# Eight of sixteen input chunks transposed early into DRAM and read back

## The chip, the cores and the metric

One core of a Trainium2 chip runs the kernel. Its engines work side by side: TensorE (PE) multiplies matrices into eight banks of PSUM, VectorE (DVE) and ScalarE (ACT) compute elementwise and copy banks to SBUF, GpSimd (POOL) and SyncE (SP) issue transfers, which run on 16 shared DMA engines. Each engine takes its instructions in order and waits at one whose inputs are not there. The metric is device time in microseconds (us); lower is better.

## The reference

Two sequence models stand side by side, each on 2048 positions of 1024 channels in bf16; their outputs are concatenated.

```python
# A: long convolution
k_shift = sum over t of k_pad[:, t:t+S, :] * shift_k[:, ks-1-t]     # ks = 4
kv = k_shift * v
y = irfft(rfft(kv) * rfft(ssm_k))[:S] + kv * ssm_D
a = q * y
# B: diagonal state space
Bu = einsum("bld,pd->blp", x, B_bar)          # complex, P = 1024 states
h[t] = Lam_bar * h[t-1] + Bu[t]
b = 2 * einsum("blp,dp->bld", h, C).real + x * Dskip
out = concatenate([a, b], axis=-1)
```

## The kernel before

Everything is emitted by one list, `ORDER`: some 1500 words such as `U.6.0.0:a30p2`. A loop takes them one by one, calls the function of that name with the numbers, and hands it slots: `a` is a unit of an arena of 53 units in SBUF (2 KB per partition each), `p` a PSUM bank, `w` a slot for the transform matrices, `h` a slot for the state. A word's engine takes it after all earlier words of that engine; a slot that is given again is waited for until its last reader is through. So the list fixes the order on each engine, the order in SP's and POOL's DMA queues, and when buffers come free. Below, "PE work between two words" is counted from the PE words that stand between them in the list.

Part B works on 16 chunks of 128 positions.

- `x.i` (line 449) reads chunk i by a transposing DMA from SP's queue, 256 KB, so that channels lie on the partitions.
- `U.i.jp.jl` (line 461) multiplies it with the prepared B: 16 matmuls of 128x128 per word, eight words per chunk. `ue.i.jp` (466) copies the bank to SBUF.
- `r1.i` (479), `r2.i` (486) rotate the input into a real recurrence, `cy.i` (488, ACT) carries the last state of chunk i-1 over, `sc.i.a` (492) scans, `r3.i` (479) and `r4.i` (498) rotate back; all but `cy` are on DVE. `cy.i` needs `r4` of chunk i-1.
- `y.i.dh.part` (508 and 511) multiplies with C and adds the skip through x: four matmuls of 512 columns and one of 128. Chunk i of x is thus read twice: by U, and at the end by y. `ye` (517) copies out, `yst` (519, POOL) or `ysp` (520, SP) stores.

Before chunk 0 the matrix B is transposed on PE (`bl` loads, `bT` line 421, `bc` line 437) and C partly there (`cl`, `cT`, `cc`), partly by transposing DMA (`cx`, line 443). `eo`, `stt`, `z1`, `z2` and the words up to `exp2` build the rotation tables.

Part A is a two-stage Fourier transform over DRAM scratch. `kp`, `vp` (526 to 534) load k and v; `kvm`, `kva`, `kvb`, `kvc` (543 to 558, DVE) make kv; `am` (563) and `ae` (569) transform 16 pieces, `ast` (572, POOL) stores them. The same for ssm_k: `hl` (578) loads, `hT` (587) transposes on PE, `hc` (592) and `hm` (609), `he` (617), `hst` (620, POOL). Then, for 16 pairs of frequencies: `lw` (624) loads matrices, `lh` and `lk` (629) read the scratch, `sh`, `sk` (640), `she` (649), `ske` (656), `sw` or `swp` (660: a swap of partitions by DMA, from POOL or SP), `pr` (666, DVE: the product), `sa` (678), `sae` (686), `vst` (689, POOL). At the end `vl` (694) reads back, `qp` (699) loads q, `a3` (706) and `a3e` (713) finish, `qm` (715, DVE) multiplies by q, `ost` (716, POOL) or `osp` (717, SP) stores. A copy whose word ends in `v` (`uev`, `shev`, ...) runs on DVE instead of ACT.

The words of part A fill the gaps of part B; both run through the whole kernel.

Of the kernel before, what the change touches and what calls it, by code (L numbers as in the profile page):

```python
# [66 lines left out]
ORDER = """  # L67
bl.0.1:a46 ld_par ld_w:a0 wb.3:p0 wbe.3:a20 bl.6.0:a32 par_T:p2 p32 exp1 dd wb.6:p4 wbe.6 wb.2:p2 ld_F wbe.2 kp.0:a12
bl.7.1:a42 bl.6.1:a43 wb.1:p1 bl.0.0:a35 wb.7:p3 wbe.7 wbe.1 wb.0:p7 bT.6.0:p4 gz x.1:a48 kring bc.6.0 wbe.0
bl.7.0:a25 kp.1 wb.5:p1 wbe.5 wb.4:p5 bl.1.0:a9 bT.0.1:p4 dve2 dve3 tabA1:a4a40a6a10 wbe.4 exp2 kp.-1 bT.6.1:p1  # L70
bT.0.0:p2 x.0:a49 bc.0.1 bT.7.1:p3 bl.2.1:a42 sm_pre sin0 bT.7.0:p5 rt bc.6.1 bc.0.0 bl.3.1:a24 tabA2 bl.1.1:a33
kvm.3:a26 U.1.3.0:a34p6 bT.1.0:p4 par_rest kva.3 U.1.0.0:p2 bc.7.1 bc.7.0 U.1.3.1 U.0.3.0:a8p0 U.0.3.1 kvm.1:a44
bT.2.1:p5 sin2 bl.2.0:a43 bl.3.0:a50 sin1 bT.3.1:p7 eo bc.1.0 kvb.3:a39 bT.1.1:p3 U.0.0.0:p1 bc.2.1 bl.5.0:a30 kva.1
kvm.2:a0 stt bl.5.1:a31 kva.2 bT.2.0:p4 bl.4.1:a38 bc.1.1 bT.3.0:p5 bl.4.0:a52 ue.0.3 U.1.0.1 U.0.0.1 bc.2.0 bc.3.0
bT.4.1:p3 bT.5.0:p0 ue.1.0 bT.4.0:p5 kp.-2 U.1.1.0:p2 bc.3.1 kvm.0:a26 bT.5.1:p4 bc.5.0 bc.4.1 kvb.1:a38 kva.0 bc.4.0
cl.2.0:a32 bc.5.1 ue.0.0 U.1.1.1 U.0.1.0:p0 x.2:a51 cT.2.0:p7 kvb.2:a36 ue.1.3 U.0.1.1 U.0.2.0:p4 vp.0:a42 U.0.2.1
cc.2.0 kvb.0:a37 ue.0.1 z1 U.1.2.0:p3 ue.0.2 U.2.1.0:a30p1 U.2.1.1 ue.2.1 cl.0.0:a24 cx.5.1 kvc.1 am.1.1:p5p6
ae.1.0.1:a28 U.1.2.1 vp.1:a6 ae.1.1.1 kvc.0 ue.1.2 U.2.3.0:p5 cl.3.1:a52 cl.1.0:a33 cT.0.0:p0 am.0.1:p1p7 ue.1.1
r1.0:a0 z2 cc.0.0 hl.1.0:a44 U.2.2.0:p2 U.2.2.1 kvc.3 ae.0.0.1:a40 r2.0:h1 ae.0.1.1 ue.2.2 kvc.2 U.2.3.1 sc.0.0
am.0.0:p3p4 kp.2 cl.2.1:a42 cl.3.0:a50 hl.1.1 sc.0.1 cT.2.1:p6 x.3:a9 r1.1:a4 ae.0.1.0 r3.0:a24 cT.3.1:p7 cT.3.0:p4  # L80
U.2.0.0:p0 cc.3.1 cc.2.1 hl.0.1:a0 U.2.0.1 cx.7.1 ae.0.0.0 hl.0.0 cl.1.1:a52 cc.3.0 cx.7.0 r2.1:h0 U.3.0.0:a10p1 ast.0
r4.0 am.1.0:p2p7 lw.0:w0 cx.4.0 cl.0.1:a32 ue.2.0 U.3.1.0:p6 cx.4.1 hT.0.5:p3 U.3.1.1 ue.2.3 ae.1.1.0 cT.1.1:p4
hc.0.5:a50 U.3.3.0:p3 ae.1.0.0 hT.0.2:p0 ue.3.1 am.2.0:p5p2 cc.1.1 cy.1 r1.2:a4 hT.0.7:p7 hT.0.0:p6 U.3.2.0:p4
hc.0.2:a8 cT.0.1:p0 ae.2.0.0:a34 hc.0.0:a52 U.3.0.1 sc.1.0 ld_Q ld_sd:a37 sc.1.1 ast.1 cx.5.0 kp.3 hT.0.1:p5 hT.0.4:p6
U.3.3.1 cc.0.1 cx.6.0 r2.2:h2 ue.3.0 ae.2.1.0 U.3.2.1 hc.0.7:a38 hm.0.2.0:p1p0 hc.0.4:a43 hm.0.2.1:p2p7 ue.3.3
cT.1.0:p6 cx.6.1 he.0.2.0.0:a40 ue.3.2 r3.1:a24 cc.1.0 hc.0.1:a8 he.0.2.1.0 he.0.2.1.1 y.0.1.0:p3 y.0.1.1 hd.0 y.0.1.2
hm.0.0.1:p4p6 hm.0.0.0:p5p2 hT.0.3:p1 y.0.1.3 r4.1 he.0.0.0.1:a26 y.0.0.0:p2 he.0.0.0.0 he.0.2.0.1 hT.0.6:p7 cy.2
he.0.0.1.1 hst.0.0.0 hst.0.2.1 he.0.0.1.0 y.0.0.1 am.2.1:p6p4 kvm.4:a30 hc.0.3:a2 hst.0.2.0 hst.0.0.1 hc.0.6:a25
ae.2.0.1 y.1.0.0:p5 sc.2.1 ae.2.1.1 kvm.5:a4 ye.0.1:a24 sc.2.0 y.0.0.2 hm.0.3.1:p0p1 he.0.3.1.1:a0 vp.2:a28
hm.0.4.0:p6p4 hm.0.3.0:p7p3 kva.5 he.0.4.0.0:a2 he.0.3.1.0 lw.3:w2 y.0.0.3 kva.4 ye.0.0 kp.4 ast.2 hst.0.3.1 r3.2:a44  # L90
x.4:a52 y.1.0.1 kvb.5:a36 he.0.4.0.1 he.0.3.0.1 he.0.3.0.0 y.1.0.2 hm.0.4.1:p2p3 hm.0.5.1:p4p6 he.0.5.1.1:a26 r4.2
he.0.4.1.1 hm.0.7.1:p1p7 he.0.7.1.1:a40 y.1.0.3 kvb.4:a42 y.1.1.0:p0 he.0.4.1.0 he.0.5.1.0 ye.1.0:a49 ysp.0 y.1.1.1
hm.0.5.0:p4p2 he.0.5.0.1 kvm.8:a44 r1.3:a4 he.0.5.0.0 hm.0.6.0:p3p6 he.0.6.0.0:a34 y.1.1.2 kva.8 he.0.6.0.1 y.1.1.3
y.2.0.0:p3 am.3.0:p6p5 ae.3.1.0:a30 y.2.0.1 r2.3:h1 hm.0.7.0:p2p5 he.0.7.1.0 he.0.7.0.1 hm.0.6.1:p7p4 kvc.4 ae.3.0.0
hst.0.3.0 kvc.5 hst.0.7.1 kvb.8:a4 he.0.6.1.1 he.0.6.1.0 ye.1.1 hst.0.4.0 cy.3 yst.1 y.2.0.2 y.2.0.3 hst.0.6.1
ye.2.0:a48 hst.0.6.0 he.0.7.0.0 vp.4:a10 sc.3.0 y.2.1.0:p6 y.2.1.1 am.3.1:p5p0 hst.0.4.1 ae.3.0.1 y.2.1.2 y.2.1.3
sc.3.1 hst.0.5.0 am.4.1:p2p4 x.5:a34 ae.4.1.1:a6 hst.0.7.0 ye.2.1 ae.3.1.1 U.4.0.0:a32p7 U.4.3.0:p5 am.5.1:p1p0
kvm.6:a0 U.4.3.1 ae.5.0.1:a28 vp.3:a40 U.4.0.1 kvc.8 ast.3 ue.4.3 am.4.0:p1p3 ue.4.0 ae.4.1.0 ae.5.1.1 r3.3:a44
U.4.2.0:p4 kva.6 am.5.0:p3p5 U.4.2.1 ae.5.0.0 ae.4.0.0 am.8.1:p7p6 ae.4.0.1 am.8.0:p0p3 ae.8.1.0:a4 U.4.1.0:p1 r4.3
kvb.6:a35 yst.2 hst.0.5.1 ue.4.2 kvc.6 U.4.1.1 ae.8.1.1 ae.8.0.1 U.5.1.0:a30p3 kvm.9:a46 U.5.1.1 ae.5.1.0 y.3.1.0:p2  # L100
y.3.0.0:p6 am.6.1:p4p5 ast.4 y.3.0.1 kvm.7:a24 ue.5.1 am.6.0:p7p3 ae.6.1.0:a6 ue.4.1 ae.8.0.0 ae.6.1.1 ae.6.0.1
y.3.0.2 kva.9 y.3.0.3 kva.7 y.3.1.1 hm.0.1.1:p3p1 he.0.1.1.1:a38 hm.0.1.0:p4p5 he.0.1.0.1 ye.3.0:a35 he.0.1.1.0
he.0.1.0.0 ae.6.0.0 y.3.1.2 kvb.9:a36 kvb.7:a51 kvc.9 hl.3.1:a42 y.3.1.3 hl.3.0 ye.3.1 hl.2.1:a0 hl.2.0 U.5.2.0:p1
am.9.1:p6p3 ae.9.0.1:a8 ae.9.1.1 U.5.2.1 ue.5.2 hT.1.3:p2 kvc.7 ast.5 hc.1.3:a50 kp.5 r1.4:a46 am.7.0:p6p5 hT.1.0:p7
hst.0.1.0 ae.7.0.0:a32 ae.7.1.0 ast.6 kvm.11:a24 ast.8 am.9.0:p0p4 ae.9.1.0 r2.4:h0 kva.11 hc.1.0:a28 hT.1.1:p1
hT.1.5:p6 am.7.1:p5p2 hc.1.1:a29 ae.7.1.1 cy.4 sc.4.0 kvb.11:a40 U.5.3.0:p3 ysp.3 hd.1 ae.7.0.1 U.5.0.0:p4 ae.9.0.0
# [16 lines left out]
ast.12 ae.13.0.0:a48 ae.13.1.0 sc.5.1 ue.7.2 kvb.14:a24 U.7.3.0:p1 U.7.3.1 kvc.15 ue.7.3 ae.13.1.1 am.15.0:p3p0 kvc.14
am.15.1:p7p4 ae.15.1.1:a4 ae.15.0.0 ae.15.1.0 r3.5:a12 x.10:a52 r4.5 U.9.2.0:a32p1 r1.6:a20 ae.15.0.1 r1.7:a28
U.9.3.0:p6 am.14.1:p3p2 U.9.3.1 am.14.0:p7p4 r2.6:h2 ae.14.1.1:a16 ysp.4 ae.14.0.1 y.5.0.0:p0 ae.14.0.0 y.5.1.0:p7
lh.0:a0 y.5.1.1 U.9.2.1 ae.14.1.0 y.5.1.2 y.5.0.1 ae.13.0.1 ast.10 sh.7:p2p5 cy.6 ast.15 ue.9.3 ue.9.2 sh.2:p6p1
# [64 lines left out]
def full_kernel(ctx, tc, A_q, A_k, A_v, A_shift_k, A_ssm_k, A_ssm_D, B_x, B_Lre, B_Lim, B_Bre, B_Bim,  # L191
# [255 lines left out]
    def x_(i):  # L447
        st["xT", i] = sb(1).rearrange("p (d t) -> p d t", d=ND)
        nc.sync.dma_start_transpose(st["xT", i], x[i * T:(i + 1) * T, :])
# [332 lines left out]
```

## Time and profile before

| | |
|---|---|
| three runs | 357.69, 358.66, 360.29 us; median 358.66 |
| the profiled execution | 358.65 us, of which 356.8 are the span of its instructions |
| granted clock of TensorE | 0.99 |
| busy: PE, DVE, ACT, POOL | 333.2, 330.3, 271.5, 68.9 us |
| DMA | 100.91 MB, mean 283 GB/s |

The page lists busy time by engine, by fortieths of the span and by line. A busy PE is not PE at its peak: the rows of its instructions overlap, so its pace is read from the starts of dense rows. The clock is a share of full speed; the chain of waits follows the last instruction back to what released it. "SPq" is SP's DMA queue.

### The profile page before, as it was taken

What the parts mean: (1) busy time and instruction counts of PE and PEld (TensorE: products, weight loads), DVE (VectorE), ACT (ScalarE), POOL (GpSimd) and SP (SyncE); (2) the same over time, 40 slices, a digit from 0 to 9 for tenths busy, and PEclk for the clock granted to TensorE, in tenths of its full rate; (3) what the DMA queues carried; (4) which work ended last, traced back from release to release, by engine and by line L of the source; (5) the groups of instructions that cost most, each with busy time, mean ns of one, the idle gap of its engine ahead of it and who ended that gap; (6) DMA issues with size and microseconds to landing.
All of it is one profiled execution on the core that took longest, in us unless ns stands there. A gap on an engine that the chain in (4) does not pass through costs nothing.

```text
span 356.8 us, 9113 instructions
## 1 busy us (share of the span) xinstructions
PE 333.2 (93%) x3745; PEld 223.9 (63%) x3785; DVE 330.3 (93%) x277; ACT 271.5 (76%) x512; POOL 68.9 (19%) x108
## 2 busy tenths in 40 slices
...
GB/s 224 326 279 310 248 242 281 194 253 44 298 294 317 282 260 177 193 312 222 348 246 311 305 303 275 317 366 320 359 303 344 319 314 327 296 355 386 204 401 154
DMA packets 62565, 100.91 MB, mean 283 GB/s; under 512 B 29438, under 2 KB 31502, under 8 KB 62524
## 3 DMA queue, kind: packets, MB, share of 16 engines
...
q0 software_dynamic: 9840, 33.74, 26.0%
...
HBM read 52.08 MB, written 33.55 MB: 240 GB/s over the span
## 4 chain that ended last, share of the span: by engine, by line
PE 70%; DMA 12%; ACT 7%; issue 5%; SPq 3%; POOL 1%; DVE 1%; POOLq 0%; DVEq 0%
PE bank L508 25%; PE bank L461 24%; PE bank L640 4%; PE bank L678 4%; DMA arena<-in_B_x_dram 3%; DMA wslot<-a_c_W 3%; PE bank L706 3%; PE bank L563 3%; SPq L443 3%; ACT BT L437 2%; PE bank L609 2%; PE bank L511 2%; DMA arena<-Vs 2%; DMA CT<-in_B_C_im_dram 2%; PE bank L421 1%
## 5 line engine op out<-in xcount | busy, mean ns | idle before, releaser
L461 PE MATMUL bank<-arena,BT 128*128 128x128 bf16 x2048 | 129.2, 222 | 5.1 <-DMA arena<-in_B_x_dram 3.5
L461 PEld LDWEIGHTS <-BT 128*128 128x128 bf16 x2048 | 120.1, 99 | 19.5 <-issue 7.7
L508 PE MATMUL bank<-CT,gslot 128*128 128x512 bf16 x483 | 120.5, 379 | 3.0 <-issue 1.0
L492 DVE TENSOR_TENSOR_SCAN gslot<-rtab,gslot 128x1040 bf16<-128x1040 f32 x32 | 73.0, 2312 | 6.3 <-ACT gslot L488 6.2
L508 PEld LDWEIGHTS <-gslot 128*128 128x128 bf16 x512 | 44.5, 98 | 53.0 <-issue 8.7
L466 ACT CAST arena<-bank 128x512 bf16<-128x512 f32 x64 | 38.7, 623 | 19.5 <-PE bank L461 17.5
L569 ACT CAST arena<-bank 128x512 bf16<-128x512 f32 x64 | 35.9, 620 | 8.9 <-PE bank L563 8.7
L617 ACT CAST arena<-bank 128x512 bf16<-128x512 f32 x64 | 34.3, 616 | 6.9 <-PE bank L609 5.9
L666 DVE TENSOR_TENSOR arena<-arena 128x4096 bf16<-128x4096 bf16 x16 | 36.6, 2287 | 2.1 <-DMA arena<-arena 1.0
L479 DVE TENSOR_TENSOR arena<-arena,Z 128x4096 bf16<-128x4096 bf16 x16 | 36.5, 2284 | 1.1 <-ACT arena L466 1.1
L479 DVE TENSOR_TENSOR arena<-gslot,Z 128x4096 bf16<-128x4096 bf16 x16 | 36.6, 2286 | 0.4
L686 ACT CAST arena<-bank 128x512 bf16<-128x512 f32 x60 | 33.4, 610 | 4.4 <-PE bank L678 4.3
L656 ACT CAST arena<-bank 128x512 bf16<-128x512 f32 x58 | 33.0, 614 | 2.6 <-PE bank L640 2.4
L649 ACT CAST arena<-bank 128x512 bf16<-128x512 f32 x57 | 31.5, 615 | 4.4 <-PE bank L640 4.4
L620 POOL DMA_DIRECT2D Ys_h<-arena x32 | 23.3, 730 | 45.8 <-ACT arena L617 45.8
L517 ACT CAST arena<-bank 128x512 bf16<-128x512 f32 x31 | 18.8, 606 | 15.6 <-PE bank L511 15.6
L543 DVE TENSOR_TENSOR arena<-arena 128x4096 bf16<-128x4096 bf16 (+3 forms) x16 | 30.1, 1884 | 0.4 <-ACT arena L466 0.3
L511 PE MATMUL bank<-Dd,arena 128*128 128x128 bf16 x128 | 28.0, 219 | 0.2
L572 POOL DMA_DIRECT2D Ys_kv<-arena x16 | 11.2, 719 | 84.2 <-ACT arena L569 82.2
L660 POOL DMA_DIRECT2D arena<-arena x16 | 8.8, 553 | 82.9 <-ACT arena L649 44.9
L713 ACT CAST arena<-bank 128x512 bf16<-128x512 f32 x24 | 12.8, 597 | 12.1 <-PE bank L706 10.9
L511 PEld LDWEIGHTS <-arena 128*128 128x128 bf16 x128 | 12.5, 98 | 15.1
(102 smaller groups left out, 383.3 us busy)
## 6 DMA issues: line engine op xcount, KB each, us to landing
...
Ys_h<-arena POOLq DMA_DIRECT2D x32, 256.0 KB, 4.0
...
```

The costliest lines, as they stand in the source:

```text
L461: nc.tensor.matmul(pu[:, w, jl, :], BT[:, 2 * jp + jl, w, d, :], xT[:, d, :], start=(d == 0), stop=(d == ND - 1))
L466: either("ue", lambda cp, i, jp: cp(st["u", i][:, :, 2 * jp:2 * jp + 2, :], st.pop(("pu", i, jp))))
L479: nc.vector.tensor_mul(m, s_, win(Z))
L492: nc.vector.tensor_tensor_scan(gf, rtab[:].rearrange("p j t -> p (j t)"), gf, 0.0, ALU.mult, ALU.add)
L508: nc.tensor.matmul(py, h[:, w, j, 2:GW], CT[:, j, w, dh * 512:(dh + 1) * 512], start=(j == 0 and w == 0), stop=False)
L511: nc.tensor.matmul(py[:, part * P:(part + 1) * P], st["xT", i][:, d, :], Dd[:, d, :], start=False, stop=(part == 3))
L569: cp(st["ysb", n2][:, p, dh * 512:(dh + 1) * 512], st.pop(("pa", n2, p, dh)))
L617: cp(o, st.pop(("pb", hf, s, e, r)).rearrange("p (n c t) -> p n c t", n=2, c=2))
L649: cp(st["hab", i][:, 0, a, l, :], st.pop(("ps", "h", g, l)))
L656: cp(st["x16", i][:, a, l, :], st.pop(("ps", "k", g, l)))
L666: nc.vector.tensor_mul(hab, st.pop(("x16", i)).rearrange("p a l d -> p (a l d)").unsqueeze(1).to_broadcast([P, 2, 2 * D]), hab)
L686: cp(st["vsb", i][:, a, dh * 512:(dh + 1) * 512], st.pop(("pv", g, dh)))
```

## The change

For chunks 8 to 15 the transposing read `x.i` writes a buffer that is only stored, by `xs.i` on POOL's queue, to a DRAM scratch of its own. Later `xl.i` on SP's queue reads it back plainly, 256 KB, into the slot that U and y read. `x.i` and `xs.i` stand early in the list, `xl.i` shortly before chunk i. Chunks 0 to 7 are read as before. All words of `ORDER` have a new place and new slots; the arithmetic is the same. Eight `xl` and eight `xs` come in; four swaps and six y stores move from SP to POOL and two stores of the last stage the other way; 28 copies of banks run on DVE instead of 26.

```diff
+    bounced = set(map(int, re.findall(r"\bxl\.(\d+)", ORDER)))
+    xd = {i: tc.dram_tile([P, D], BF16, name="xd%d" % i) for i in sorted(bounced)}
+
     def x_(i):
+        nm = "xm" if i in bounced else "xT"
+        st[nm, i] = sb(1).rearrange("p (d t) -> p d t", d=ND)
+        nc.sync.dma_start_transpose(st[nm, i], x[i * T:(i + 1) * T, :])
+    E["x"] = x_
+    E["xs"] = lambda i: gpd(xd[i], st.pop(("xm", i)).rearrange("p d t -> p (d t)"))
+
+    def xl(i):
         st["xT", i] = sb(1).rearrange("p (d t) -> p d t", d=ND)
-        nc.sync.dma_start_transpose(st["xT", i], x[i * T:(i + 1) * T, :])
-    E["x"] = x_
+        spd(st["xT", i].rearrange("p d t -> p (d t)"), xd[i])
+    E["xl"] = xl
```

Of the list, the places that the prediction speaks of; the old ones first:

```diff
...
-ast.7 kvm.10:a24 hst.0.1.1 sc.4.1 U.5.0.1 U.5.3.1 hc.1.5:a41 hm.1.1.0:p5p2 kva.10 hm.1.1.1:p0p7 x.8:a11 ue.5.0 kp.6
-x.9:a36 U.8.0.0:a6p1 he.1.1.1.0:a46 hT.1.4:p0 hT.1.7:p6 he.1.1.0.1 U.8.3.0:p4 ue.5.3 hc.1.4:a51 he.1.1.1.1 vp.5:a48
-x.6:a10 he.1.1.0.0 U.8.3.1 kvc.11 hT.1.2:p0 hc.1.7:a29 hT.1.6:p3 hm.1.7.0:p7p5 kvb.10:a37 he.1.7.0.1:a32 he.1.7.0.0
-hc.1.2:a3 U.8.1.0:p2 U.8.1.1 ue.8.3 r3.4:a42 U.8.0.1 am.11.0:p6p5 U.6.1.0:a38p7 ae.11.1.0:a4 U.6.1.1 hc.1.6:a35 ue.8.0
...
-a3ev.10.0 ysp.13 r3.15:a10 a3ev.3.0 r4.15 a3.11.0:p7 a3.1.1:p5 a3.15.0:p3 a3.1.0:p4 a3.5.0:p6 ye.14.0:a42 a3e.15.0
-qm.1 a3ev.11.0 a3ev.5.0 y.15.1.0:p3 a3.12.1:p0 a3ev.12.1:a10 qm.5 a3.13.0:p1 a3ev.1.1 a3e.1.0 a3.13.1:p2 a3.0.0:p7
-qm.7 qm.2 a3e.0.0 a3e.13.1 a3e.13.0 y.15.1.1 a3.12.0:p0 ost.5 y.15.1.2 a3.8.0:p5 ost.2 y.15.0.0:p6 y.15.1.3 a3e.12.0
-a3.9.1:p0 a3.9.0:p4 a3.8.1:p1 qm.0 a3e.8.0:a28 a3e.8.1 a3e.9.1 qm.6 osp.1 y.15.0.1 a3ev.9.0 y.15.0.2 y.14.1.0:p1 ost.0
-qm.4 y.15.0.3 yev.15.0:a3 osp.7 ye.15.1 osp.6 y.14.1.1 ost.4 y.14.1.2 y.14.1.3 ysp.15 ye.14.1 yst.14
...
+he.0.5.0.1 ye.0.1 hm.0.4.0:p3p2 kp.4 kvc.5 r3.2:a0 hst.0.2.0 hst.0.2.1 yst.0 x.13:a11 hst.0.0.1 hm.0.4.1:p7p1
+hm.0.0.0:p0p6 he.0.4.1.0:a48 he.0.4.1.1 y.1.1.0:p5 y.1.0.3 he.0.4.0.0 kvm.8:a42 he.0.0.0.0 vp.4:a40 r4.2 y.1.1.1
+he.0.0.0.1 hm.0.5.1:p0p7 hm.0.7.0:p1p6 he.0.4.0.1 hst.0.0.0 kva.8 kvm.9:a0 y.1.1.2 he.0.5.1.0 x.4:a28 he.0.7.0.0
+hst.0.6.0 y.1.1.3 he.0.5.1.1 he.0.7.0.1 kva.9 hst.0.7.0 U.4.2.0:a36p2 hst.0.4.1 kvb.8:a38 x.5:a29 hst.0.5.1 kvb.9:a25
...
+hm.1.0.0:p6p2 he.1.0.0.0:a48 lw.0:w1 he.1.0.1.1 hm.1.1.1:p4p1 he.1.1.1.1 he.1.0.0.1 U.5.0.0:p3 hT.1.3:p6 hc.1.3:a51
+ye.3.0 x.10:a8 U.5.0.1 vp.5:a24 kvc.11 xs.10 he.1.1.1.0 ue.5.0 lw.1:w2 kp.6 ast.7 he.1.0.1.0 sc.4.0 sc.4.1 kvc.10
+hT.1.5:p1 hc.1.5:a33 hT.1.6:p5 U.8.2.0:a10p2 U.8.2.1 ue.8.2 hc.1.6:a32 U.8.0.0:p0 hT.1.7:p3 hc.1.7:a8 am.11.1:p6p7
+ae.11.1.1:a44 ae.11.0.1 hT.1.2:p4 U.8.0.1 ue.8.0 am.11.0:p5p1 ae.11.0.0 hc.1.2:a9 ae.11.1.0 U.8.1.0:p2 U.8.1.1 ue.8.1
+U.8.3.0:p3 hm.1.3.1:p4p1 he.1.3.1.0:a40 yst.3 r1.5:a0 hm.1.7.1:p5p7 he.1.7.1.1:a38 hm.1.7.0:p0p6 he.1.7.0.0 he.1.7.1.0
+hst.1.0.0 he.1.7.0.1 x.6:a27 U.6.0.0:a30p2 U.6.0.1 ue.6.0 ast.11 he.1.3.1.1 hst.1.0.1 hm.1.3.0:p5p4 he.1.3.0.0 r3.4:a4
...
+sh.7:p0p4 sh.6:p6p7 yst.4 sh.2:p5p1 she.2.0 U.9.3.0:p2 U.9.3.1 r1.7:a17 she.6.0:a4 she.6.1 r4.6 sw.0.0 y.5.0.3
+U.9.1.0:p5 r2.7:h1 U.9.1.1 ye.5.0 ue.9.3 she.2.1 she.7.1 sk.2:p6p2 cy.7 ue.9.1 ske.2.1:a24 sw.1.0 sw.1.1 sk.3:p7p1
+ske.3.1 y.6.1.0:p3 y.6.1.1 y.6.0.0:p2 y.6.1.2 swp.0.1 ske.3.0 sc.7.1 ske.2.0 sc.7.0 she.7.0 lk.0:a10 sk.0:p4p6 pr.1
...
+sae.27.0:a45 qp.6:a38 sa.26:p0p5 sae.26.1 sae.26.0 sae.27.1 vst.13 y.12.1.1 y.12.1.2 y.12.1.3 ye.12.1:a11 qp.0:a50
...
+ue.15.3 sc.14.1 sc.14.0 a3.11.0:p2 y.13.1.1 a3.7.0:p4 a3.7.1:p6 U.15.1.1 y.13.1.2 a3e.7.0:a28 a3.10.1:p4 y.13.1.3
...
+y.14.1.3 a3.8.0:p6 a3.3.0:p4 vl.1:a32 ye.12.0 vl.9:a46 a3e.12.1 y.14.0.1 qm.6 y.14.0.2 r3.15:a20 qp.4:a34 r4.15
+a3.1.1:p0 a3e.3.1 osp.2 ye.14.1:a10 a3e.3.0 a3e.8.0:a16 osp.6 qm.1 yst.12 a3.0.0:p4 osp.1 a3e.1.1:a44 a3.1.0:p5
+a3.0.1:p7 a3ev.1.0 a3.8.1:p6 a3ev.0.1 a3e.0.0 qm.0 a3.9.0:p3 a3ev.9.0 qm.5 osp.5 a3ev.8.1 ost.0 y.14.0.3 ye.14.0
+ysp.14 a3.9.1:p1 a3ev.9.1 qm.4 ost.4 y.15.1.0:p4 y.15.1.1 y.15.1.2 y.15.1.3 yev.15.1:a52 y.15.0.0:p0 y.15.0.1 y.15.0.2
+y.15.0.3 ye.15.0 yst.15
```

213 lines of the change are left out of this document (102 added, 111 removed).

## The prediction

> **What bounds the kernel now.** I read the page's busy shares first, then busy time by stretch, then who waits for whom, then the chain that ended last around the one long transfer in it, and last the rows of single lines.
>
> ```profile
> span 356.8 us, 9113 instructions
> PE 333.2 (93%) x3745; PEld 223.9 (63%) x3785; DVE 330.3 (93%) x277; ACT 271.5 (76%) x512; POOL 68.9 (19%) x108
> ```
>
> Two engines are nearly full, TensorE (PE) and VectorE (DVE). The stretches say where each has room (columns: us, then busy us of PE, PEld, DVE, ACT, POOL, the granted clock, the DMA share, GB/s):
>
> ```profile
> 60.00:120.00 60.00, 58.33 (x559) 36.17 (x566) 58.09 (x47) 46.99 (x88) 16.11 (x23) 1.00 0.75 239
> 120.00:140.00 20.00, 16.42 (x241) 14.82 (x240) 19.49 (x18) 14.20 (x26) 3.57 (x5) 0.91 0.94 240
> 140.00:180.00 40.00, 39.47 (x463) 27.27 (x467) 38.73 (x29) 32.67 (x67) 14.82 (x21) 1.00 0.78 250
> 180.00:240.00 60.00, 59.37 (x636) 34.77 (x645) 56.28 (x31) 48.79 (x100) 7.09 (x12) 1.00 0.96 309
> 240.00:300.00 60.00, 58.84 (x779) 37.96 (x786) 57.73 (x39) 53.93 (x109) 14.06 (x23) 1.00 0.93 325
> 300.00:335.00 35.00, 33.94 (x274) 19.79 (x276) 34.58 (x22) 15.61 (x31) 1.88 (x3) 1.00 0.90 328
> ```
>
> From 140 to 335 us PE is idle 3.4 us (195 less 191.6), DVE 7.7 us. PE sets the pace there; a PE stall before 140 is not won back. There is one, at 120 to 140: 3.6 us idle at a clock of 0.91. DVE is idle 10.1 us from 60 to 335.
>
> ```profile
> PE bank L461 <- DMA arena<-in_B_x_dram: 3.5, 2, 3.3
> DVE gslot L492 <- ACT gslot L488: 6.2, 6, 2.7
> 122.53 12.00 DMA arena<-in_B_x_dram
> 134.58 3.53 PE L461 MATMUL bank<-arena,BT 128*128 128x128 bf16 x32 [3.29 <-DMA arena<-in_B_x_dram]
> 138.44 1.95 PE L461 MATMUL bank<-arena,BT 128*128 128x128 bf16 x32
> 114.85 1.48 SPq L449 DMA_TRANSPOSE arena<-in_B_x_dram  x1
> 117.11 4.74 SPq L449 DMA_TRANSPOSE arena<-in_B_x_dram  x1
> 122.53 1.85 SPq L449 DMA_TRANSPOSE arena<-in_B_x_dram  x1
> L449 SPq DMA_TRANSPOSE arena<-in_B_x_dram x16: 1231/1721/5196, 4.9 to 286.7; - x16
> DMA to landing us min/median/max: 5.8/7.1/8.0
> ```
>
> The three L449 rows are x.8, x.9 and x.6, in the order's sequence. x.9 is not read until chunk 9, yet it holds SP's queue 4.74 us, and x.6 goes out behind it and takes 12.0 us. PE stands 3.29 us for x.6, and its next 32 matmuls take 3.53 us instead of 1.95, at half clock.
>
> **The change, part by part.**
>
> *The stall.* In the new order x.8 and x.9 leave this place; chunk 8 comes by xl.8, x.6 follows x.10, vp.5, lw.1 and kp.6, and its slot 27 is freed by hm.1.1.1. Between hm.1.1.1 and U.6.0.0 PE has nine U halves, five hT, two am and three hm.
>
> ```profile
> 93.00 1.79 PE bank L461 x32
> 67.19 0.56 PE bank L609 x8
> 115.19 0.52 PE bank L587 x8
> 336.55 0.86 PE bank L508 x4
> 337.41 0.06 PE bank L511
> 326.40 1.94 PE bank L706 x9
> ```
>
> A U half is 16 matmuls, 0.9 us; an hT 8 transposes of L587, 0.52; an am two, 0.43 (as L706: 1.94/9 each); an hm four of L609, 0.28. Together 9x0.9 + 5x0.52 + 2x0.43 + 3x0.28 = 12.4 us of cover, as long as the longest landing seen (12.0). So the wait goes: -3.29, and the half clock with it: -(3.53 - 1.95) = -1.58. Bounds: 0 (it comes back whole) to -4.87. I take -4.87.
>
> *The reloads.* Eight xl read 256 KB plainly. No such load exists yet; the nearest rows are other 256 KB transfers:
>
> ```profile
> arena<-in_B_B_im_dram SPq DMA_DIRECT2D x8, 256.0 KB, 5.0
> arena<-in_B_B_re_dram SPq DMA_DIRECT2D x8, 256.0 KB, 6.3
> arena<-in_B_C_im_dram SPq DMA_DIRECT2D x4, 256.0 KB, 3.1
> L520 SPq DMA_DIRECT2D out_dram<-arena x10: 344/399/1474, 76.4 to 349.5; - x10
> L519 POOL DMA_DIRECT2D out_dram<-arena x6: 570/576/637, 89.2 to 352.4; - x6
> ```
>
> 3.1 to 6.3 us to land; I take 5.0. xl.8 is the tightest: its slot is freed by kvb.7, with about 8 us of PE work before U.8.2.0; the others have 9 us and more. Cost on the path 0 (0 to 1 each if they land late). SP issues 176 words before and after: eight xl (0.35 each) come, and fewer swaps and y stores, so its queue is not fuller. The eight xs and eight more swaps and stores go to POOL, 16x0.58 = 9.3 us on an engine busy 19%; 0. Each xs waits for its transpose, and behind it on POOL stand stores of kv and h pieces; the worst is ast.7, some 6 us late behind xs.10; its slot is next written by ue.6.0, about 11 us of PE work after that. 0, up to +2.
>
> *DMA.* 8x2x256 KB = 4.2 MB, at the mean 283 GB/s 14.8 us of all engines' time. By their places in the order six of the eight transposes go out between 60 and 180 us, where the share is 0.75 to 0.94, and late five plain reads replace five transposes. 0, and 14.8 at the most if all of it showed.
>
> ```profile
> DMA packets 62565, 100.91 MB, mean 283 GB/s; under 512 B 29438, under 2 KB 31502, under 8 KB 62524
> ```
>
> *A new tight spot.* x.4 had some 20 us of PE work from slot to use. Now slot 28 is freed by hm.0.0.0, and before U.4.2.0 stand five y quarters (0.92 each) and two hm (0.56): 5.2 us. At the median landing of 7.1 PE waits 7.1 - 5.2 = +1.9. Bounds: 0 (PE is itself late) to 12.0 - 5.2 = +6.8.
>
> *The turn into the last stage.* Now PE waits 0.79 us for the first V read, and the last V store (vst.13) stands about 5 us of PE work ahead of it, in the new order 13. So -0.79 (0 to -0.79).
>
> ```profile
> 313.58 0.60 PE L706 MATMUL bank<-arena,Gt 128*128 128x512 bf16 x2 [0.79 <-DMA arena<-Vs]
> 333.92 1.22 DVE L498 TENSOR_TENSOR gslot<-arena 128x2048 bf16<-128x2048 bf16 x1
> 351.24 0.22 PE L511 MATMUL bank<-Dd,arena 128*128 128x128 bf16 x1
> L715 DVE TENSOR_TENSOR arena<-arena 128x2048 bf16<-128x2048 bf16 x8 | 9.5, 1219 | 0.7 <-ACT arena L713 0.7
> L713 DVE CAST arena<-bank 128x512 bf16<-128x512 f32 x8 | 5.4, 683 | 0.5 <-PE bank L706 0.5
> ```
>
> *VectorE and the tail.* DVE evacuates 28 banks instead of 26: +1.4 us (2x0.683), hidden in its idle time where PE is the bound, +1.4 where not. Behind the last r4 (L498, ending at 335.1) stand now seven qm and six evacuations, 12.6 us; in the new order four and six, 9.0. So 3.6 + 1.4 = 5.0 us more of DVE work lie ahead of the last r4. PE's work behind it falls alike, from 14 a3 and 12 y quarters (17.1 us) to 7 and 9 (11.3).
>
> *The start.* Loads, transposes and evacuations are reshuffled; up to r1.0 DVE has the same work, PE 5 us less, ACT about the same. 0, within 2 either way.
>
> The sum by PE, against the profiled execution's own 358.65 us (1.85 over its span; the median of the runs is 358.66, so the same): 358.65 - 4.87 - 0.79 + 1.9 = **354.9**. The sum by DVE: last r4 at 335.1 + 5.0, less the idle time d that DVE saves, then at most 11.3 of PE, 5.4 from PE's end (351.46) to the span's, and 1.85: 358.7 - d; up to 4 less where PE does the a3 ahead of time. d: the first scan of a chunk waits for the carry cy, which needs the r4 of the chunk before (the L492 row above, 6.2 us). Chunks with under 3 us of DVE work between that r4 and the scan: 1, 2, 7, 15 now, 2 and 7 then. Half of 6.2 is 3.1, which puts this sum at 351.6 to 355.6, around the other. I keep 354.9.
>
> A rule of the Trainium skill speaks against the change ("SBUF — State Buffer", section "SBUF: two separate sides"): a DMA issued from POOL can be starved by VectorE's work, its issue growing from some 620 ns to some 3100. The L519 row says 570 to 637 ns beside a DVE that is 93% busy, so the trace doesn't show it; by the rule each of the 16 moved or added issues would cost an estimated 2.5 us more of POOL.
>
> **The rivals.**
> 1. *Both engines follow fully*: x.4 costs nothing and d is all 6.2. 358.65 - 4.87 - 0.79 = 353.0, by DVE 352.5. I give it 352.8. For it: longer DVE cover at chunks 1, 3, 15. Against: shorter at 5, 6, 7, 10.
> 2. *DVE is the bound; the PE stall was hidden anyway*, the bounce buys nothing: d = 0, 358.7. For it: DVE was 19.49 of 20 us busy while PE stood. Against: its 7.7 us idle after 140.
> 3. *The stall only moves to x.4*: it lands as late as x.6 did, behind x.13: 358.65 - 4.87 - 0.79 + 6.8 + 1.58 = 361.4. For it: x.13 is two places ahead in SP's queue. Against: x.13 can go out some 8 us earlier. It decides from a landing of 10.9 us on.
> 4. *The vector waits grow* (slower): cy of chunk 7, the longest wait now (2.7), keeps only r2.7 (1.22 us) as cover and stands behind two evacuations of sh banks on ACT; if the scans' waits double, d = -6.2: 358.7 + 6.2 = 364.9. It decides when DVE's idle time from 60 to 335 exceeds today's 10.1. Against: two chunks are short of cover, not four.
> 5. *POOL's issues stretch*: the four swaps moved to POOL each 2.5 us late on DVE's products, 354.9 + 10 = 364.9. Against: 637 ns at most. This is the skill's rule, above, as it would act here.
>
> **How the numbers follow.** Forecast 0.42 (own range 353 to 357.5), rival 1 0.20, rival 2 0.15, rival 3 0.09, rival 4 0.12, rival 5 0.02. One per cent is 3.6 us, about what a measurement here tells from no change; the line is 355.1. Faster: rival 1 and 0.25 of the forecast, 0.45. Slower beyond 362.2: rivals 4 and 5 and 0.03 of the third, 0.17. The rest, 0.38, within. The range reaches from 351 (rival 1 with its engines a little better still) to 362 (the third in it); rivals 4 and 5 are left out, and some 0.05 below.
>
> **What would show it.** Right: no PE wait for in_B_x near 130 us and one half-clock stretch less; a PE wait of about 2 us before U.4; the waits of L492 near 3.1 us; no wait of L706 for Vs; POOL's issues still under 0.7 us. Wrong: DVE idle 10 us or more from 60 to 335 with the last r4 after 340 us (rival 2 or 4); a PE wait of over 5 us before U.4 (3); POOL rows of 2 us and more (5); or a new PE wait for an xl.

## The result, and the profile after

The kernel after takes 358.26 us (median of 20 runs, 356.0 to 361.0); the kernel before, beside it, 357.80 (20 runs, 352.9 to 363.9). The ratio after to before is **1.0079, 95% interval 1.0051 to 1.0108**: some 0.8% slower, where 1% faster was forecast. No gain shows: the ratio leaves out runs more than 1.5% above a kernel's fastest, which drops seven long runs of before and none of after; over all runs the medians are 0.46 us apart. After's worst run is better than before's, and its best is worse. The profiled execution took 359.87 us, its span is 358.1.

The page's head and busy shares:

```profile
span 358.1 us, 9158 instructions
...
PE 332.1 (93%) x3746; PEld 220.8 (62%) x3785; DVE 331.9 (93%) x279; ACT 270.7 (76%) x510; POOL 77.1 (22%) x124
```

VectorE has two evacuations more, POOL sixteen DMAs. Three stretches, in the columns of the prediction:

```profile
120.00:140.00 20.00, 19.46 (x297) 16.19 (x298) 19.96 (x15) 19.61 (x36) 5.50 (x8) 1.00 0.75 258
...
180.00:240.00 60.00, 56.51 (x589) 31.48 (x594) 57.20 (x34) 46.49 (x95) 12.12 (x20) 1.00 0.91 317
...
300.00:335.00 35.00, 33.35 (x275) 20.13 (x277) 30.50 (x20) 14.61 (x29) 1.45 (x2) 1.00 0.89 310
```

From 120 to 140 us PE has 19.46 of 20 us at full clock, where it had 16.42 at 0.91: the stall is gone. From 180 on both engines are emptier: PE idles 3.5 us from 180 to 240 (0.6 before), DVE 4.5 from 300 to 335 (0.4 before). In the second profiles (e2 and e1 below) it is 1.4 against 0.8, and 4.7 against 0.6. Who waits for whom in after (us in total, times, longest):

```profile
DVE arena L726 <- ACT arena L726: 2.3, 1, 2.3
DVE arena L679 <- DMA arena<-Ys_kv: 2.2, 1, 2.2
PE bank L691 <- DVE arena L679: 2.1, 2, 1.3
PE bank L653 <- DMA wslot<-a_c_W: 1.9, 2, 1.1
DVE arena L492 <- DMA Vs<-arena: 1.8, 1, 1.8
DVE arena L679 <- DMA arena<-arena: 1.4, 1, 1.4
PE bank L719 <- DMA arena<-Vs: 1.2, 1, 1.2
```

No engine that computes waits for in_B_x or for a reload. In their place stand a kv reload (L679 is pr), a swap, weights (lw), a V store that frees r1.14's units (L492), V reads, and evacuations of a3 behind those reads (L726): late transfers of the last two stages.

Four instants split both runs: the first r1 starts, the last sa group ends, the last matmul ends, the program ends behind POOL's DRAIN. After, then before:

```profile
38.37 2.29 DVE L492 TENSOR_TENSOR arena<-arena,Z 128x4096 bf16<-128x4096 bf16 x1 [1.21 <-ACT arena L479]
299.00 1.06 PE L691 MATMUL bank<-arena,wslot 64*64 64x512 bf16 x16
351.75 0.22 PE L524 MATMUL bank<-Dd,arena 128*128 128x128 bf16 x1
```

```profile
37.60 2.29 DVE L479 TENSOR_TENSOR arena<-arena,Z 128x4096 bf16<-128x4096 bf16 x1 [1.11 <-ACT arena L466]
299.88 1.06 PE L678 MATMUL bank<-arena,wslot 64*64 64x512 bf16 x16
```

The longest of POOL's three DRAINs (shortest, median and longest in ns; first and last start in us), after and before; it is the first of the three:

```profile
L790 POOLq DRAIN  x3: 51/107/4423, 352.9 to 357.8; - x3
```

```profile
L777 POOLq DRAIN  x3: 51/99/3702, 352.4 to 356.6; - x3
```

With the last matmul of before from the prediction's row (351.24 + 0.22), and the same rows of the three profiles that follow among the experiments, in us:

| profile | first r1 | to last sa | to last matmul | to the end |
|---|---|---|---|---|
| before | 37.6 | 263.3 | 50.5 | 5.3 |
| before, again | 37.3 | 266.5 | 50.9 | 5.4 |
| before, x.6 first | 37.3 | 261.8 | 51.1 | 5.4 |
| after | 38.4 | 261.7 | 51.9 | 6.1 |
| after, again | 39.9 | 259.6 | 52.3 | 6.1 |

The long middle part fell by 1.6 us from the first profile of before to the first of after, and by 6.9 between the second ones, as meant. Around it the new order is longer: by 0.8 and 2.7 at the start, by 1.4 behind the last sa (there it has nine U halves left, 0.9 us each, the old one eight), by 0.7 to 0.8 behind the last matmul. And one word moved in the old order (x.6 first) brings the middle to 261.8 without any of it.

### The profile page after: what moved, and what is told of

It is laid out like the page before. It is cut to its first block, busy times and chain, and to the rows that moved or that the text cites. A ratio compares the mean times of both kernels' runs of the same rounds, so it can differ in the third digit from the quotient of the medians.

```text
span 358.1 us, 9158 instructions
## 1 busy us (share of the span) xinstructions
PE 332.1 (93%) x3746; PEld 220.8 (62%) x3785; DVE 331.9 (93%) x279; ACT 270.7 (76%) x510; POOL 77.1 (22%) x124
## 4 chain that ended last, share of the span: by engine, by line
issue 17%; PE 16%; DVE 10%; DMA 6%; POOL 2%; ACT 2%; POOLq 0%; SPq 0%; DVEq 0%
PE bank L521 8%; DVE arena L679 4%; PE bank L474 4%; DMA arena<-arena 3%; DVE arena L492 3%; PE bank L653 2%; PE bank L691 2%; DMA arena<-Ys_kv 2%; DMA wslot<-a_c_W 1%; DVE gslot L505 1%; ACT arena L662 1%; POOL Vs L702 1%; DVE gslot L511 1%; POOL out_dram L729 0%; PE bank L524 0%
## 5 line engine op out<-in xcount | busy, mean ns | idle before, releaser
L474 PE MATMUL bank<-arena,BT 128*128 128x128 bf16 x2048 | 126.9, 220 | 1.5 <-ACT BT L439 0.6
L474 PEld LDWEIGHTS <-BT 128*128 128x128 bf16 x2048 | 117.8, 98 | 16.1 <-issue 11.1
L479 ACT CAST arena<-bank 128x512 bf16<-128x512 f32 x59 | 36.0, 628 | 19.3 <-PE bank L474 16.6
L582 ACT CAST arena<-bank 128x512 bf16<-128x512 f32 x64 | 35.8, 631 | 8.2 <-PE bank L576 7.3
L679 DVE TENSOR_TENSOR arena<-arena 128x4096 bf16<-128x4096 bf16 x16 | 36.4, 2284 | 4.0 <-DMA arena<-Ys_kv 2.2
L492 DVE TENSOR_TENSOR arena<-arena,Z 128x4096 bf16<-128x4096 bf16 x16 | 36.5, 2283 | 3.2 <-DMA Vs<-arena 1.8
L669 ACT CAST arena<-bank 128x512 bf16<-128x512 f32 x62 | 35.4, 620 | 5.3 <-PE bank L653 5.2
L699 ACT CAST arena<-bank 128x512 bf16<-128x512 f32 x60 | 34.2, 631 | 3.7 <-PE bank L691 3.7
L492 DVE TENSOR_TENSOR arena<-gslot,Z 128x4096 bf16<-128x4096 bf16 x16 | 36.6, 2288 | 0.3
L630 ACT CAST arena<-bank 128x512 bf16<-128x512 f32 x64 | 34.5, 613 | 3.2 <-PE bank L622 2.8
L662 ACT CAST arena<-bank 128x512 bf16<-128x512 f32 x56 | 30.9, 610 | 7.6 <-PE bank L653 4.8
L530 ACT CAST arena<-bank 128x512 bf16<-128x512 f32 x31 | 18.3, 605 | 18.3 <-PE bank L524 18.2
L673 POOL DMA_DIRECT2D arena<-arena x20 | 10.9, 547 | 62.9 <-ACT arena L662 42.3
L653 PE MATMUL bank<-arena,wslot 64*64 64x512 bf16 x256 | 20.2, 386 | 1.9 <-DMA wslot<-a_c_W 1.9
```

What stands on the lines that cost most here:

```text
L474: nc.tensor.matmul(pu[:, w, jl, :], BT[:, 2 * jp + jl, w, d, :], xT[:, d, :], start=(d == 0), stop=(d == ND - 1))
L479: either("ue", lambda cp, i, jp: cp(st["u", i][:, :, 2 * jp:2 * jp + 2, :], st.pop(("pu", i, jp))))
L492: nc.vector.tensor_mul(m, s_, win(Z))
L582: cp(st["ysb", n2][:, p, dh * 512:(dh + 1) * 512], st.pop(("pa", n2, p, dh)))
L630: cp(o, st.pop(("pb", hf, s, e, r)).rearrange("p (n c t) -> p n c t", n=2, c=2))
L662: cp(st["hab", i][:, 0, a, l, :], st.pop(("ps", "h", g, l)))
```

## Experiments

Seventeen runs were made, two of them of the unchanged kernels, each timed beside runs of before on the same chip; ratios are to before. Two theories to begin with: A, the stall for x.6 belongs to the one execution profiled; B, the stall is real, and the bounce's traffic gives its gain back. Later ones stand in the expectations.

**Both kernels again** (e1, e2). No edit.

> The kernel before, unchanged, profiled once more. Theory A (the 4.87 us that TensorE lost on x.6 belong to the one execution that was profiled): the new profile shows less than 1 us of waiting for in_B_x near 130 us and TensorE near 330 us busy. Theory B (the loss belongs to the kernel): 3 to 5 us of waiting for in_B_x there again, at a similar place.

> The kernel after, unchanged, profiled once more. If the waits of its first profile (lk 2.2 us, the V store 1.8, the swap 1.4, two weight loads 1.9, the V read 1.2) belong to the kernel, at least three of the five come back at the same instructions with 1 us or more; if they are chance, other places show and the sum of vector waits for DMA stays below 3 us.

Before: 357.96 us (10 runs), ratio 0.998 (0.993 to 1.004). After: 359.1 (10 runs), 1.006 (1.003 to 1.009). The second profile of before has the stall again:

```profile
37.26 2.29 DVE L479 TENSOR_TENSOR arena<-arena,Z 128x4096 bf16<-128x4096 bf16 x1 [0.78 <-ACT arena L466]
136.56 3.19 PE L461 MATMUL bank<-arena,BT 128*128 128x128 bf16 x32 [2.47 <-DMA arena<-in_B_x_dram]
302.67 1.06 PE L678 MATMUL bank<-arena,wslot 64*64 64x512 bf16 x16
354.38 0.22 PE L511 MATMUL bank<-Dd,arena 128*128 128x128 bf16 x1
```

2.5 us, a little under the 3 to 5 of theory B, and again slow matmuls behind it (3.19 us for 32, against 1.95): A falls. (This execution took 361.75 us, its span is 360.0.) In the second profile of after (span 357.9) three of the five waits came back with 1 us or more, so these belong to the kernel:

```profile
PE bank L719 <- DMA arena<-Vs: 1.6, 1, 1.6
...
DVE arena L679 <- DMA arena<-Ys_kv: 1.5, 1, 1.5
DVE arena L492 <- DMA Vs<-arena: 1.5, 1, 1.5
```

```profile
39.94 2.29 DVE L492 TENSOR_TENSOR arena<-arena,Z 128x4096 bf16<-128x4096 bf16 x1 [2.79 <-ACT arena L479]
298.43 1.06 PE L691 MATMUL bank<-arena,wslot 64*64 64x512 bf16 x16
351.53 0.22 PE L524 MATMUL bank<-Dd,arena 128*128 128x128 bf16 x1
```

It has all 3785 matmuls on record, where the first profiles lack some 40 and so show TensorE a little emptier than it is. It tells how full the kernel is (60 to 335 us):

```profile
60.00:335.00 275.00, 271.34 (x3024) 171.26 (x3019) 265.39 (x182) 211.05 (x415) 68.46 (x105) 1.00 0.93 303
```

**The stall alone** (e3).

```
-... x.8:a11 ue.5.0 kp.6 x.9:a36 U.8.0.0:a6p1 ... vp.5:a48 x.6:a10 he.1.1.0.0 ...
+... x.8:a11 ue.5.0 kp.6 U.8.0.0:a6p1 ... vp.5:a48 x.6:a10 x.9:a36 he.1.1.0.0 ...
```

> The kernel before with one word moved: x.9 is issued behind x.6 instead of two places ahead of it. Theory A (the stall is not in the usual run): same as before within 1 us, 0 to -1. Theory B (the stall is in every run and TensorE sets the pace there): 3 to 5 us faster, some 354. Theory C (VectorE hides it): the wait is gone from the profile and the time is the same within 1 us.

355.78 us (12 runs, 353.8 to 358.4) against 358.04 of before (29 runs, 354.3 to 365.4); ratio 0.9965 (0.9927 to 1.0004). The wait is gone (span 355.6):

```profile
37.33 2.29 DVE L479 TENSOR_TENSOR arena<-arena,Z 128x4096 bf16<-128x4096 bf16 x1 [0.82 <-ACT arena L466]
136.57 1.95 PE L461 MATMUL bank<-arena,BT 128*128 128x128 bf16 x32
298.08 1.06 PE L678 MATMUL bank<-arena,wslot 64*64 64x512 bf16 x16
349.97 0.22 PE L511 MATMUL bank<-Dd,arena 128*128 128x128 bf16 x1
```

By the medians 2.3 us, and the longest time is 7.0 us below that of before; the interval of the ratio just reaches 1. So the stall is real and on the path, and worth about half of the 4.87 us that one profile showed.

Where the stall reaches VectorE, the traces tell. Some 50 us behind it a scan waits for its carry, 2.75 us in the first profile of before and 2.74 in the second; in e3 it does not wait. Before, then e3:

```profile
185.97 4.54 DVE L492 TENSOR_TENSOR_SCAN gslot<-rtab,gslot 128x1040 bf16<-128x1040 f32 x2 [2.75 <-ACT gslot L488]
```

```profile
184.50 4.53 DVE L492 TENSOR_TENSOR_SCAN gslot<-rtab,gslot 128x1040 bf16<-128x1040 f32 x2
```

In e7 below, where TensorE idles 3.8 us between 120 and 140 us, mostly for other reasons, this scan waits 2.75 us again; in e8 and e17 (2.2 and 2.3 us idle) it waits 1.8 and 1.0; in e12 and e16 (under 0.5) it does not wait. That the stall costs what it makes this scan wait is inferred from the nearness of 2.75 to 2.3, not shown.

**The new order without the bounce** (e4).

```
-... x.8:a6 ... xs.8 ... xl.8 ...     (and so for 9 to 15)
+... x.8 at xl.8's place, transposing, with xl.8's unit ...
```

> The kernel after in its own order, but without the bounce: the eight early transposes and the eight stores to the scratch are left out, and each xl is a transposing load of x at xl's place. Theory B (the 4.2 MB more and POOL's sixteen more issues make the later loads, swaps and stores late): the waits for lk, lw, the swap and the V store shrink to under 4 us together, and it is 2 to 5 us faster than after, unless a transpose is late at its U half (then a wait for in_B_x of 2 us or more stands there). Theory D (the order makes those waits, not the bounce): the same waits, and the time of after within 1.5 us.

360.96 us (6 runs), 1.0149 (1.0081 to 1.0217): by the medians 1.9 slower than after (359.1, e2). VectorE's waits at pr and at r1.14 stand there, pr's now for a swap:

```profile
189.15 2.29 DVE L677 TENSOR_TENSOR arena<-arena 128x4096 bf16<-128x4096 bf16 x1 [2.55 <-DMA arena<-arena]
```

pr waits 4.1 us for swaps in all, r1.14 1.8 for the V store, TensorE 0.2 for weights: 6.1 where theory B has under 4, and the kernel is not faster. So theory B falls for the new order: the order makes VectorE's waits. The V reads were there sooner without the bounce (0.4 us of waiting, not 1.2). By the medians the bounce is worth something within this order, though the intervals of e2 and e4 overlap.

**The bounce in the old order**: dense (e6), spread (e9), spread without x.15 (e16), and that with the end of e12, below (e17).

```
-... x.8:a11 ... x.9:a36 ... x.15:a52 ...
+... x.8:a43 (early, in a free unit) ... xs.8 ... xl.8:a11 ...  (and so for 9 to 15)
```

> The order of before with the bounce alone: x.8 to x.15 are transposed some 75 to 110 us into the run, in units of the arena that are free there, each is stored some 11 us later, and a plain reload stands where each x stood; no other word is moved. Theory E (the bounce is good, the new order gives its gain back): no wait for in_B_x at x.6, and as fast as the kernel with x.6 issued first, 354.5 to 356.5. Theory B (the 4.2 MB and the sixteen further transfers cost by themselves): the stall goes, but other waits for DMAs grow by 2 us or more and the time is 357 to 360.

> The bounce alone in the order of before once more, with the eight early transposes spread out: one every 6 to 22 us of TensorE work (68, 82, 88, 112, 133, 141, 147 and 161 us of it), not eight within 18, each stored 8 to 12 us later, all other words where they were. Theory E (the bounce is good; SP's queue, held by the dense transposes, made the earlier trial slow): no wait for a v load over 1 us, no wait for in_B_x at x.6, and 354.5 to 357. Theory B (the extra traffic costs by itself): 358 or more with DMA waits that stand at no transpose.

Dense: 369.81 us (6 runs), 1.031 (1.024 to 1.037). SP's queue, then VectorE:

```profile
95.52 12.11 SPq L454 DMA_TRANSPOSE arena<-in_B_x_dram  x5
107.82 0.43 SPq L546 DMA_DIRECT2D arena<-in_A_v_dram  x1
```

```profile
116.77 0.69 DVE L570 TENSOR_TENSOR arena<-arena 128x1024 bf16<-128x1024 bf16 x1 [9.01 <-DMA arena<-in_A_v_dram]
```

Five transposes in a row hold SP for 12.11 us, 2.4 each; a v load goes out behind them and VectorE stands 9 us. Spread: 360.44 us (6 runs), 1.015 (1.010 to 1.021). The v loads are in time, but the early x.15 waits for its unit, and the kv reloads (L642) stand behind it on SP until 183.25 us (177.25 with x.6 first):

```profile
181.72 1.23 SPq L455 DMA_TRANSPOSE arena<-in_B_x_dram  x1
183.25 0.89 SPq L642 DMA_DIRECT2D arena<-Ys_kv  x2
```

```profile
188.50 0.41 PE L653 MATMUL bank<-arena,wslot 64*64 64x512 bf16 x4 [3.20 <-DMA arena<-Ys_kv]
```

Both were faults of my placing, so neither theory was settled by them.

> The spread bounce in the order of before, with x.15 left a direct transpose at its old place (its early form held the kv reloads for 6 us); x.8 to x.14 bounced as before. Theory E (the bounce does what it is meant to; only its placing cost): no wait for the kv reloads near 188 us and none for x.6, and 355 to 357, level with x.6 first. Theory B (it costs by itself): 358 or more, with waits for DMAs that no single transpose stands ahead of.

> The same with the five last output stores on SP's queue. By e12 and e14 it should be 1.2 to 1.6 us faster than without: 353.5 to 356 by theory E, 356.5 or more by theory B. Level with e12 (354.25) it would show that the bounce buys nothing over one moved word.

e16: 359.26 us (12 runs), 0.999 (0.995 to 1.003), before on that chip 358.97. e17: 357.42 (12 runs), 0.996 (0.991 to 1.001). No wait for the kv reloads and none for x.6 is left in e16, yet it is level with before: theory E's 355 to 357 is missed by 2 us, and theory B's mark of 358 is reached. One new wait, of TensorE for an x among the early transposes, is 1.34 us (at 107.81). But the execution profiled took 363.22 us, and VectorE's longest wait in it is another:

```profile
73.70 2.32 DVE L505 TENSOR_TENSOR_SCAN gslot<-rtab,gslot 128x1040 bf16<-128x1040 f32 x1 [6.53 <-ACT gslot L501]
```

It stands ahead of the first early transpose (x.8, issued at 82.11 us), behind TensorE, which stands 2.84 us at 65.35 at its first matmul with C. The same scan waits in the old order too, 1.76 us in the first profile of before, 4.85 in the second, 4.67 in e3, 2.40 in e17; in after all scans together wait 0.2. So the old order has a second wait whose size changes from execution to execution, and part of e16's time may be that.

Taking the stall away by one moved word gained 2.3 us by the medians, taking it away by the bounce nothing (the intervals of e3 and e16 overlap). Whether the bounce's transfers eat the gain, and which, was not found.

**Work off VectorE**, in after (e5) and in an improved old order (e8).

```
-... skev.11.1 ... uev.11.0 ... uev.11.2 ... shev.18.1:a8 ...
+... ske.11.1 ... ue.11.0 ... ue.11.2 ... she.18.1:a8 ...
```

> The kernel after with four evacuations of chunks 11 to 18's stretch (skev.11.1, uev.11.0, uev.11.2, shev.18.1; 0.68 us each on VectorE) done by ScalarE instead, nothing else changed. If VectorE sets the time (rival 2): its last r4 comes 2.7 us earlier and the time falls by 2 to 3 us below after. If TensorE or the late DMAs set it: the time stays within 1 us and VectorE's idle time between the first r1 and the last r4 grows by the 2.7 us.

362.19 us (6 runs), 1.013 (1.008 to 1.019): not faster, and by the medians 3 to 4 us slower than after, which neither theory has. The old order first got cx.6.0 and cx.6.1 ahead of cl.1.1 (e7), then the like edit to saev.27.0, a3ev.7.0, a3ev.10.0 and a3ev.3.0:

```
-... cl.1.1:a52 ... kp.3 ... cx.6.0 ... cx.6.1 ...
+... cx.6.0 cx.6.1 cl.1.1:a52 ... kp.3 ...
```

> The kernel with x.6 ahead of x.9, and cx.6.0 and cx.6.1 moved ahead of cl.1.1 on SP's queue, into its idle time near 44 us. In both new profiles of the old order a transpose of C landed late near 65 us (TensorE 2.3 to 2.4 us, the scan behind it 4.7 to 4.9). If that wait is on the path that sets the end: it goes and the time falls by 2 to 4 us below the kernel with x.6 first, some 352 to 354. If VectorE catches up behind it, the same within 1 us. If the later loads of C, pushed back by some 3 us, are now late: a wait of ScalarE or TensorE for them of 2 us or more.

> The kernel of the run before this one with four evacuations of VectorE (saev.27.0, a3ev.7.0, a3ev.10.0, a3ev.3.0, all ahead of the last r4) done by ScalarE instead. If VectorE sets the time: 2 to 2.7 us faster than without. If not: the same within 1 us.

356.23 us (12 runs; 0.996, 0.991 to 1.000) and 357.32 (12 runs; 1.000, 0.996 to 1.004). In e7 a load of C behind the moved ones is late instead, and the scan behind it still waits 4.39 us, so the price of that wait was not measured:

```profile
60.29 0.66 PE L421 MATMUL bank<-ident,arena 128*128 128x128 bf16 x8 [3.70 <-DMA arena<-in_B_C_im_dram]
```

VectorE's work shrank as planned and its time did not come back. Busy us from 60 to 335 us, after and then e5 (third count is VectorE):

```profile
60.00:335.00 275.00, 266.66 (x2960) 169.46 (x2994) 263.76 (x180) 209.39 (x411) 67.42 (x104) 1.00 0.92 303
```

```profile
60.00:335.00 275.00, 268.29 (x3007) 169.29 (x3002) 260.19 (x176) 211.51 (x416) 68.69 (x105) 1.00 0.92 299
```

Its idle time rose from 11.2 us (9.6 in the second profile of after) to 14.8, more than the 2.7 taken away. VectorE alone does not set the time.

**VectorE's new waits taken away**, in after (e10).

```
-... pr.1 ... r3.7:a20 ... r1.14:a44 ... a3ev.14.0:a4 ... a3ev.7.1 ...
+... r3.7:a20 pr.1 ... r1.14:a6 ... a3e.14.0:a4 ... a3e.7.1 ...
```

> The kernel after with the three largest waits of VectorE for late DMAs taken away, each by what makes it: pr.1 goes behind r3.7 (2.2 and 1.5 us in the two profiles), r1.14 writes units 6 to 9 instead of 44 to 47, so that it waits for no V store (1.8 and 1.5), and a3ev.14.0 and a3ev.7.1, which wait for late V reads ahead of r1.15 (2.3 and 2.9), go to ScalarE, which also takes 1.3 us of work off VectorE. Theory F (these new waits ate the gain): 4 to 7 us faster than after, 352 to 355. Theory G (the waits are slack that moves on to the next late transfer): less than 2 us faster, and VectorE's idle time from the first r1 to the last r4 still 9 us or more.

359.48 us (6 runs), 1.012 (1.006 to 1.017). Theory G: nothing won, and r1.15 now waits for the a3 that the late V reads hold up:

```profile
321.95 2.29 DVE L492 TENSOR_TENSOR arena<-arena,Z 128x4096 bf16<-128x4096 bf16 x1 [2.85 <-PE bank L719]
```

**The start**, in after: z2 later (e11), then also the load of bl.7.1 earlier and two banks exchanged (e13).

```
-... bl.3.1:a31 ... bl.7.1:a4 ... bT.0.0:p6 ... bT.0.1:p7 ... z2 ... ue.0.2 ...
+... bl.3.1:a31 bl.7.1:a4 ... bT.0.0:p7 ... bT.0.1:p6 ... ue.0.2 z2 ...
```

> The kernel after with z2 (three casts of ScalarE, 3.0 us, not needed before r3.0) moved from ahead of ue.0.2 to behind it; in the order of before it stands behind r1.0. VectorE's first r1 waited 1.2 and 2.8 us for that ue. If the start is part of the price of the new order: the first r1 at 37.0 to 37.6 us instead of 38.4 and 39.9, and the time 1 to 2.5 us below after. If the start is slack: the first r1 earlier, and the same time within 0.7 us.

> The kernel after with its start mended: z2 behind ue.0.2 as before, bl.7.1 loaded right behind bl.3.1 (TensorE waited 1.9 to 2.4 us for it), and bT.0.0 and bT.0.1 change banks (bT.0.0 waited 1.2 us for ScalarE to empty bank 6). If TensorE's start is the price of the new order: its idle time before the first r1 falls from 9.2 to 10.4 us to about 7.5, and the time by 2 to 3 us below after. If not: the idle time comes back behind the start, and the time stays within 1 us.

359.63 and 359.64 us (12 runs each); 1.011 (1.007 to 1.016) and 1.013 (1.009 to 1.017). In e11 the first r1 starts at 37.23 us without a wait, and a later r1 takes the wait over:

```profile
37.23 2.29 DVE L492 TENSOR_TENSOR arena<-arena,Z 128x4096 bf16<-128x4096 bf16 x1
...
55.87 2.29 DVE L492 TENSOR_TENSOR arena<-arena,Z 128x4096 bf16<-128x4096 bf16 x1 [2.34 <-ACT arena L479]
```

The first r1 is slack. In e13 TensorE's waits only moved to other loads of B.

**The end**, in the old order with x.6 first (e12), in after (e14), and in after with the start of e13 (e15).

```
-... ost.0 ... ost.4 ... yst.12 ... yst.15        (after; in the old order ost.5 ost.2 ost.0 ost.4 yst.14)
+... osp.0 ... osp.4 ... ysp.12 ... ysp.15
```

> The kernel with x.6 first, with five of its last output stores (ost.5, ost.2, ost.0, ost.4, yst.14) issued by SP instead of POOL. POOL's last instruction, a DRAIN, took 3.70 us in every profile with 108 of POOL's instructions, 4.02 with 116, 4.42 with 124, and the program ends behind it. If it costs some 0.045 us for each DMA that POOL issued: 3.48 us here, and with the last store off POOL the end comes 0.3 to 1.2 us earlier after TensorE's last matmul (5.4 us before). If it is a fixed wait for the last landing: the DRAIN's end and the time stay within 0.3 us.

> The kernel after with four of its last output stores (ost.0, ost.4, yst.12, yst.15) issued by SP instead of POOL. In the old order the like edit brought the end from 5.4 to 4.2 us behind the last matmul. Here it should come from 6.1 to about 4.2, and the time 1.5 to 2 us below after, whatever holds before; under 0.7 us if POOL's DRAIN is not what ends the program.

> Both edits, start and tail, in the kernel after. If the two places are the whole gap to the old order without its stall: 3.5 to 5 us below after, 354 to 356, level with the old order with x.6 first. If only the tail counts: 1.5 to 2 us, some 357 to 358.

e12: **354.25 us** (12 runs), 0.9925 (0.9882 to 0.9967): faster than before, and by the ratios than after. e14: 357.61 (12 runs), 1.003 (0.999 to 1.007). e15: 358.4 (12 runs), 1.004 (0.999 to 1.008). The last matmul and the DRAIN in e12, then in e14:

```profile
345.84 0.22 PE L511 MATMUL bank<-Dd,arena 128*128 128x128 bf16 x1
```

```profile
L777 POOLq DRAIN  x3: 51/99/8627, 321.9 to 350.0; - x3
```

```profile
351.47 0.22 PE L524 MATMUL bank<-Dd,arena 128*128 128x128 bf16 x1
```

```profile
L790 POOLq DRAIN  x3: 51/99/6871, 329.2 to 355.4; - x3
```

The DRAIN starts some 29 and 24 us earlier and is over before the last matmul; the program ends 4.2 and 4.0 us behind that matmul (spans 350.3 and 355.7), not 5.4 and 6.1. e15, with the mended start as well, is no faster than e14.

## Why the prediction was wrong

Two steps failed. The sum by PE paid TensorE's lost 4.87 us out in full at the end, where taking the stall away is worth about half; and, x.4 aside, both sums counted the waits that go and none that the new order brings: some 6 us of VectorE's and a longer end. Term by term:

- **The stall** (-4.87). It went, as worked out, and stayed away. Mis-sized: by x.6 first it is worth 2.3 us in the median. The sum took it at the size that it had for TensorE in the one execution profiled, by the rule that a PE stall before 140 is not won back; what VectorE lost by it, as far as the traces tell, is 2.75. Its ratio in e3, 0.9965, makes it 0.35%, so the ratio of after could show little of it.
- **The reloads** (0): right. They land in 5.0 us, the value taken, and nobody that computes waits for one.

```profile
arena<-xd SPq DMA_DIRECT2D x8, 256.0 KB, 5.0
```

- **x.4** (+1.9): wrong, 0, its lower bound. No wait for in_B_x stands before chunk 4, so rival 3 falls.
- **POOL's issues** (0): right, and rival 5 with them. The swaps, the moved ones among them, take 547 ns, the xs 581, the stores of kv, h and V 700 to 734 (719 to 736 before); the slowdown in the Trainium skill ("SBUF — State Buffer", section "SBUF: two separate sides"), given there beside a copy on VectorE, does not show here either.

```profile
L673 POOL DMA_DIRECT2D arena<-arena x20 | 10.9, 547 | 62.9 <-ACT arena L662 42.3 <-ACT gslot L501 10.5 <-PE bank L653 7.5
...
L457 POOL DMA_DIRECT2D xd<-arena x8 | 4.6, 581 | 27.7 <-DMA arena<-in_B_x_dram 15.2 <-DVE arena L558 12.5
```

- **Sixteen more DMAs of POOL hidden** (0): wrong at the end of the program, where I did not look. The DRAIN took 4.42 us instead of 3.70: +0.7, in both profiles of each kernel.
- **The V read** (-0.79): wrong; it waits 1.2 us, 0.4 more than before, not none (1.6 against 1.1 in the second profiles).
- **DMA, 4.2 MB more** (0): by e4, which leaves them out, VectorE's waits at pr and at r1.14 do not come from them, while the V reads' may in part. By the medians of e16 the bounce as a whole gave back about what its stall was worth; that it was the traffic is not shown.
- **The tail and the last r4.** The last r4 starts at 340.86, 7 us later than before, where 5.0 less d, so 1.9, were forecast; the stretch behind it fell from 21.7 us (356.8 - 335.1) to 16.0, by 5.7, close to the 5.8 that the words gave.

```profile
340.86 1.23 DVE L511 TENSOR_TENSOR gslot<-arena 128x2048 bf16<-128x2048 bf16 x1
```

- **d, the idle time that VectorE saves** (+3.1): the step that failed in the DVE sum. The scans' waits fell further than forecast, from 6.2 us to 0.2 (the row below; from 8.6 to 0.2 in the second profiles). But pr, r1.14 and the evacuations of a3 took their place, with 2.2, 1.8 and 2.3 us (1.5, 1.5 and 2.9 in the second profile). What is left is not settled by one profile of each: VectorE's idle time from 60 to 335 us is 11.2 us instead of 10.1 in the first pair, 9.6 instead of 13.9 in the second. The mark named for rivals 2 and 4, DVE idle 10 us or more with the last r4 after 340, is reached in the first profile of after and missed in the second. The sum counted the waits that go and none that come.

```profile
L505 DVE TENSOR_TENSOR_SCAN gslot<-rtab,gslot 128x1040 bf16<-128x1040 f32 x32 | 73.1, 2312 | 0.2
```

- **The start** (0, within 2): the first r1 came 0.8 and 2.7 us later, in the second pair past the bound, but e11, e13 and e15 show it to be slack.

So the time came out at rival 2's (358.7), but by chance and not for its reason (rival 1 needed d at 6.2, and rival 4 the scans' waits, which shrank): VectorE as the bound would have made e5 and e8 faster. Between 60 and 335 us TensorE has 271 and VectorE 265 of 275 us in the full record of after; each waits for the other's banks and units, and in e5 and e10 what VectorE was spared it spent waiting. Only taking away the stall for x.6, which as it seems VectorE waits for in its turn, and the shorter end moved the time to the better, both by the medians.

What stays open: after lies about 3 us behind the old order with x.6 first, by the medians. The DRAIN is 0.7 of it. The one U half more behind the last sa fits a further 0.9, but that was not tried. The rest lies ahead of the last sa and at no single place of those tried; e16 suggests that the bounce itself has a part in it, e4 that in the new order it is still the better choice (1.9 us by the medians).
